# Attention with beacon keys and a maxout FFN: batch 0 cut at 512 queries, zeros between the first scores, a written order for batches 0 and 1

## The chip, the cores and the metric

The kernel runs on one core of a Trainium2 chip. Its engines are TensorE (PE, with its weight loads shown apart as PEld), VectorE (DVE), ScalarE (ACT), GpSimd (POOL) and SyncE (SP); each works through its own queue in order, and semaphores tie them together. The metric is the device time in microseconds of one execution. Beside it stands the span of one profiled execution, from its first to its last instruction.

## The reference

Two stages follow one another. Attention has 8 batches of 8 heads, 576 queries of 64 numbers, and 16 beacon keys and values that every query may see ahead of 576 causal ones:

```
k_all = np.concatenate([beacon_k, k], axis=2)
v_all = np.concatenate([beacon_v, v], axis=2)
scores = scale * np.matmul(q, k_all.transpose(0, 1, 3, 2))
scores = np.where(causal, -1000000000.0, scores)
a = softmax(scores)
attn_out = np.matmul(a, v_all)
```

The heads are then laid side by side, so that each of 4608 tokens has 512 numbers, and go through an FFN with three input matrices of 512 x 768 and one output matrix of 768 x 512:

```
h = np.maximum(np.maximum(x @ w1, x @ w2), x @ w3)
out = h @ w_out
```

Inputs and output are float32.

## The kernel before, in words

**Layout.** Matmuls are in bf16. Four heads make a quad (`HG = 4`), so there are two quads a batch and 16 in all, numbered Q. Queries and keys of a quad are loaded with a head on every 32 partitions, cast to bf16 (`cast_qk`) and transposed by DVE (`turn`, L197) into `qT` and `kT`, of which there are three each. The beacon keys of batch 0 come separately: POOL clears `first32` (L139), ACT's queue issues four small loads into it (L158), and DVE casts, transposes and copies them into `kT` (`turn_first_beacon_k`, L160). Those of batch 1 are loaded by SP after the values of batch 0 and turned by `turn_beacon_k` and `put_beacon_k`.

**Scores.** The 592 keys of a head are five tiles of 128, and a query needs only the tiles up to its own place. For each tile the columns are therefore the queries from a first one on, 1664 columns a quad. They are cut into bursts, or steps, that fill a PSUM bank of 512 columns for each of four heads. `emit_scores` multiplies a step's scores (L273; 32 rows of the array for each head, four heads at a time). ACT takes the exponential of two heads at once out of PSUM (L288, two instructions a step, which free the two `sc` tiles for the next step), and POOL zeroes what lies past the diagonal (`emit_masks`, L304). In batches 0 and 1 (`N_APART`) a quad has four steps of its own, of 496, 464, 336 and 368 columns, and in batch 0 the heads are multiplied in pairs. From batch 2 on the steps run on across quads, 3.25 a quad.

**Sums.** What this document calls the sums are the products of the exponentials with the values and, for the denominator, with a matrix of ones. In batches 0 and 1 `pv_pass` (L316) does one such product for half of the queries (288), into one of two PSUM banks; ACT turns a denominator into its reciprocal by a logarithm and an exponential (L344, L346), and DVE multiplies (scales) the two parts of the sums with it into `xT` (L350). From batch 2 on `pv_segment` does a third or two thirds of the queries at once (L387, L396 to L403).

**FFN.** A block is 512 tokens, so that block 0 consists of the first 512 of batch 0's 576 tokens. It has 18 input units of four matmuls (`mm1_unit`, L438; DVE takes the maximum over the three matrices in `hT`, L451) and then four output units of six matmuls (`mm2_unit`, L458). There are 198 units. `emit_ffn` emits the next one when the sums of its batch are done (`ready`) and the pace allows it: two a step during batch 1, 3.4 a step later.

**What sets the order.** The engines' queues hold the order in which the program emits, and this is written out: `begin` for the loads and batch 0's first quad, a table of steps (`at_step`) for loads, casts and transposes, and the loop in `emit_all` that puts scores, sums and units in turn. Before the first scores PE multiplies 17 times a matrix of zeros (`spare`, L545). In the loop, all of batch 0's sums are done at step 8 before the first FFN unit, and what is left of batch 1's before step 16 (`late`), the first of batch 2. The last output unit of all (`last_unit`) is done in two halves, whose copies and stores go over ACT and DVE with SP.

## Time and profile before

| | us |
|---|---|
| median of 3 runs | 287.48 |
| lowest, highest | 287.34, 288.59 |
| profiled execution, its own time | 286.83 |
| its span | 284.9 |
| busy: PE, DVE, ACT, POOL | 273.2, 171.4, 157.2, 88.4 |

In rows of the trace, the first two numbers are start and duration in us, counted from the first instruction. `out<-in` names what an instruction writes and reads, `x16` says that 16 of them were merged into one row, and brackets tell how long the engine had been idle before and for whom it waited. A merged row reaches from its first start to its last end, so other rows of the same engine can begin a little before it ends. In groups of instructions the columns are count, busy time in us, mean in ns, and idle time of the engine just before them with what ended it. `SPq`, `ACTq` and the like are an engine's own queue, where loads are issued. "Clock" is the share of TensorE's full clock that was granted.

### The profile page before, as it was taken

The numbers are of one execution on the slowest core, as the hardware profiler recorded it, in microseconds if no ns is written. First come the engines' busy times: TensorE is split into PE (matmuls) and PEld (weight loads), VectorE is DVE, ScalarE is ACT, GpSimd is POOL, SyncE is SP. The second block draws the span as 40 slices with busy tenths as digits, with TensorE's granted clock in tenths as the row PEclk, the third lists the DMA queues.
The fourth block names the chain that finished last, engine by engine and source line by source line (L and its number), as shares of the span: only waits on it lengthen the run. The fifth ranks groups of instructions, "written<-read, shape, count | busy, mean of one in ns | idle before, by whom it ended". The sixth has DMA issues, their size and how long they took to land.

```text
span 284.9 us, 7997 instructions
## 1 busy us (share of the span) xinstructions
PE 273.2 (96%) x3393; PEld 134.5 (47%) x3431; DVE 171.4 (60%) x298; ACT 157.2 (55%) x246; POOL 88.4 (31%) x165
## 2 busy tenths in 40 slices
PE   7699999999999999999999999999999999999995
PEld 3246444534545454445454545445454644444442
DVE  4727769856675766656656575666544465554553
ACT  5796576457784766556673686376647630210210
POOL 0483862235553523153415340442134100000000
PEclk9856999999999999999999999999999999999999
DMA  7999999689944954159056913380031003003004
GB/s 247 234 187 203 138 181 206 98 156 251 222 74 122 221 105 84 41 171 197 2 85 196 208 14 73 148 174 3 0 113 39 2 2 134 13 2 147 1 0 147
DMA packets 51923, 33.06 MB, mean 116 GB/s; under 512 B 41264, under 2 KB 42288, under 8 KB 51888
## 3 DMA queue, kind: packets, MB, share of 16 engines
q1 hardware_dynamic: 41152, 20.40, 27.6%
q0 software_dynamic: 10464, 12.01, 26.3%
q8 instruction: 26, 0.43, 0.6%
q10 hardware_dynamic: 272, 0.15, 0.2%
q14 instruction: 9, 0.07, 0.1%
HBM read 35.13 MB, written 9.44 MB: 156 GB/s over the span
## 4 chain that ended last, share of the span: by engine, by line
PE 91%; ACT 3%; issue 1%; DMA 1%; DVE 1%; ACTq 0%; DVEq 0%
PE fps L438 36%; PE sc L273 12%; PE fps L458 11%; PE pv L387 10%; PE pv L438 7%; PE sc L438 6%; PE pv L334 4%; ACT at_sb L288 3%; PE pv L458 2%; PE sc L458 2%; DMA first<-in_beacon_k_dram 1%; PE sc L387 1%; DVE xT L350 0%; ACTq L158 0%; DVE hT L451 0%
## 5 line engine op out<-in xcount | busy, mean ns | idle before, releaser
L288 ACT ACTIVATE at_sb<-sc 128x1024 bf16<-128x1024 f32 (+7 forms) x128 | 103.7, 861 | 31.8 <-PE sc L273 31.6
L438 PE MATMUL fps<-xT,w_sb 128*128 128x512 bf16 x447 | 113.3, 380 | 2.5 <-issue 1.6
L438 PEld LDWEIGHTS <-w_sb 128*128 128x128 bf16 x648 | 59.8, 98 | 74.5 <-issue 6.9
L304 POOL TENSOR_SCALAR_AFFINE_SELECT at_sb<-at_sb 128x512 bf16<-128x512 bf16 (+6 forms) x89 | 47.5, 551 | 127.4 <-ACT at_sb L288 119.0
L451 DVE TENSOR_TENSOR hT<-hT,fps 128x512 bf16<-128x512 bf16 x79 | 54.0, 685 | 33.9 <-PE fps L438 28.1
L273 PE MATMUL sc<-qT,kT 32*128 32x288 bf16 (+15 forms) x960 | 39.7, 266 | 2.9 <-ACT at_sb L288 2.5
L446 ACT CAST hT<-fps 128x512 bf16<-128x512 f32 x34 | 19.9, 586 | 29.9 <-PE fps L438 22.7
L458 PE MATMUL fps<-w_out_sb,hT 128*128 128x512 bf16 x144 | 34.7, 380 | 0.4 <-issue 0.3
L403 DVE TENSOR_TENSOR xT<-pv,recip 128x240 bf16<-128x240 f32 (+1 forms) x46 | 18.8, 450 | 25.5 <-ACT recip L398 24.9
L458 PEld LDWEIGHTS <-hT 128*128 128x128 bf16 x210 | 19.8, 98 | 25.6 <-DVE hT L451 1.7
L273 PEld LDWEIGHTS <-kT 32*128 32x128 bf16 x960 | 19.4, 94 | 22.3 <-issue 16.4
L396 ACT ACTIVATE lnd<-pv 128x240 f32<-128x240 f32 (+1 forms) x23 | 9.4, 408 | 29.8 <-PE pv L387 29.8
L466 DVE COPY y<-fps 128x512 f32<-128x512 f32 x25 | 17.3, 691 | 12.6 <-PE fps L458 12.2
L200 DVE STREAM_TRANSPOSE kT<-c 128x256 uint32<-128x256 uint32 (+1 forms) x32 | 22.0, 707 | 3.2 <-ACT c L193 3.1
L438 PE MATMUL pv<-xT,w_sb 128*128 128x512 bf16 x87 | 22.5, 379 | 0.2
L438 PE MATMUL sc<-xT,w_sb 128*128 128x512 bf16 x83 | 21.5, 380 | 0.1
L200 DVE STREAM_TRANSPOSE qT<-c 128x256 uint32<-128x256 uint32 (+1 forms) x32 | 21.5, 701 | 0.0
L387 PE MATMUL pv<-at_sb,v_sb 128*32 128x160 bf16 (+7 forms) x808 | 20.2, 243 | 0.0
L387 PEld LDWEIGHTS <-v_sb 128*32 128x32 bf16 (+1 forms) x864 | 16.3, 97 | 1.3
L226 POOL CAST v_sb<-vst 128x1024 bf16<-128x1024 f32 (+1 forms) x18 | 15.7, 894 | 0.5 <-issue 0.5
L451 DVE TENSOR_TENSOR hT<-hT,pv 128x512 bf16<-128x512 bf16 x15 | 10.3, 688 | 7.5 <-PE pv L438 4.1
L451 DVE TENSOR_TENSOR hT<-hT,sc 128x512 bf16<-128x512 bf16 x14 | 9.6, 687 | 7.6 <-PE sc L438 6.9
(54 smaller groups left out, 152.9 us busy)
## 6 DMA issues: line engine op xcount, KB each, us to landing
out_dram<-y SPq DMA_DIRECT2D x35, 256.0 KB, 2.0
vst<-in_v_dram SPq DMA_DIRECT2D x21, 256.0 KB, 4.8
c<-in_k_dram POOLq DMA_DIRECT2D x14, 288.0 KB, 4.9
c<-in_q_dram POOLq DMA_DIRECT2D x14, 288.0 KB, 6.0
w_sb<-in_moe_w_dram POOLq DMA_DIRECT2D x3, 768.0 KB, 8.6
vst<-in_v_dram SPq DMA_DIRECT2D x7, 224.0 KB, 3.5
vst<-in_v_dram SPq DMA_DIRECT2D x7, 160.0 KB, 6.9
w_out_sb<-in_moe_w_out_dram POOLq DMA_DIRECT2D x1, 768.0 KB, 10.1
```

What stands on the lines that cost most here:

```text
L200: nc.vector.transpose(dst.rearrange("p (t s) -> p s t", s=RUN)[:, s0:s1], src.rearrange("p (s d) -> p s d", d=DP),)
L226: cast(v_tiles[b][0:n, t0:t1].rearrange("p t h d -> p (t h d)"), stage["v", b][0:n, t0:t1].rearrange("p t h d -> p (t h d)"),)
L273: nc.tensor.matmul(sc[h // 2][:, h % 2, off : off + w], kT[hs, 128 * t : 128 * (t + 1), j], qT[hs, q0:q1, j], start=(j == 0), stop=(j == 1 ...
L288: nc.scalar.activation(out=at[Q][:, 2 * i : 2 * i + 2, a0 : a0 + w], in_=sc[i][:, :, off : off + w], func=AF.Exp, scale=scale,)
L304: nc.gpsimd.affine_select(out=view, in_=view, compare_op=ALU.is_ge, fill=0.0, base=q0 - (128 * t - Nb), pattern=[[0, HG], [1, edge - q0]], ...
L387: nc.tensor.matmul(pv_banks[32 * j : 32 * j + 32, c : c + w], lhsT, at_sb[0:r, j, a : a + w], start=(t == 0), stop=all(x[1] // BANK != c / ...
L403: nc.vector.tensor_mul(xT[:, 2 * g + part - 1, c0 : c0 + n], pv_banks[:, offs[part] : offs[part] + n], recip,)
L438: nc.tensor.matmul(ps[:, o0 : o0 + n], w_in[i][:, ct, 128 * ft : 128 * (ft + 1)], xT[:, ct, x0 : x0 + n], start=(ct == 0), stop=(ct == n_c ...
L446: nc.scalar.copy(hT[:, ft, :], ps)
L451: nc.vector.tensor_max(hT[:, ft, :], hT[:, ft, :], ps)
L458: nc.tensor.matmul(ps, hT[:, ft, 128 * tt : 128 * (tt + 1)], w_out_sb[:, ft, :], start=(ft == 0), stop=(ft == n_ft - 1),)
L466: nc.vector.tensor_copy(y, ps)
```

## The change

Batch 0's queries are cut at 512 (`TOKB`). Each of its two quads has three steps (`main`, 464, 496 and 384 columns) for the first 512 queries, which are all that FFN block 0 needs. The last 64 queries of both quads (`rest`, 320 columns a quad) are put into the steps behind them, which now run on without a gap through batch 1; batch 2 begins a new step. Its first step is number 14 (`N_FIRST`) instead of 16. Batch 1 uses whole quads and `pv_segment`, as the later batches do. The halves of `pv_pass` in batch 0 are 288 and 224 queries wide.

The sums of the last 64 queries of both quads are done together by a new function, `pv_rest`, in three passes (ones, then the two parts of the values) of 40 matmuls that are 64 columns wide.

All of the emission up to batch 2 is one written list. A letter stands for an action: S and E are a step's scores with its first exponential, and its second exponential with the masks; s and p a denominator and a sum of `pv_pass` (quad, half, part); r a pass of `pv_rest`; g and h a segment and its scaling; C a cast (quad, which, piece, and by ACT 0, DVE 1 or POOL 2); B and b beacon keys; t a transpose; k, v, w and n loads; c a cast of values; f the next FFN unit (with 1: its copy by DVE; with 2: in a third PSUM bank); x a number of multiplications with zeros, now 256 columns wide.

Smaller edits: `first32` is cleared by DVE; one staging buffer for values instead of two; reciprocals have a pool of four; the pace from batch 2 on starts at 22 units and is 3.2 a step instead of 3.4 once the second batch is through; the second half of the last output unit is copied half by ACT and half by DVE.

```diff
-    by_burst = [
-        [[(0, 0, HALF), (3, q_min[3], S)], [(1, q_min[1], S)], [(2, q_min[2], S)]]
-        + [[(0, HALF, S), (4, q_min[4], S)]],
-        [[(t, q_min[t], S) for t in range(n_kt)]],
-    ]
+    main = [[(0, 0, HALF), (1, q_min[1], HALF)]]
+    main.append([(2, q_min[2], HALF), (0, HALF, TOKB), (1, HALF, TOKB)])
+    main.append([(2, HALF, TOKB), (3, q_min[3], TOKB), (4, q_min[4], TOKB)])
+    rest = [[(t, TOKB, S) for t in range(n_kt)]]
+    whole = [[(t, q_min[t], S) for t in range(n_kt)]]
...
+    order = [(Q, main) for Q in range(n_quad)] + [(Q, rest) for Q in range(n_quad)]
+    order += [(Q, whole) for Q in range(n_quad, NQ)]
...
-    vst_pool = ctx.enter_context(tc.tile_pool(name="vst", bufs=2))
+    vst_pool = ctx.enter_context(tc.tile_pool(name="vst", bufs=1))
...
+    recip_pool = ctx.enter_context(tc.tile_pool(name="recip", bufs=4))
...
     for x in first32:
-        nc.gpsimd.memset(x, 0.0)
+        nc.vector.memset(x, 0.0)
...
+    def pv_rest(part):
+
+        n_r = S - TOKB
+        if part == 0:
+            bank = pv_pool[0].tile([128, 512], FP32, name="pv")[:, 0 : 3 * n_quad * n_r]
+            rest_tiles.append(bank.rearrange("p (g c n) -> p g c n", g=n_quad, c=3))
+        ps = rest_tiles[0]
+        for Q in range(n_quad):
+            for t in range(n_kt):
+                a = next(a + TOKB - q0 for q0, q1, a in at_piece[Q, t] if q0 <= TOKB < q1)
+                n = k_rows[t]
+                for j in range(HG):
...
+                    nc.tensor.matmul(
+                        ps[32 * j : 32 * j + 32, Q, part],
+                        lhsT,
+                        at[Q][0:n, j, a : a + n_r],
...
-        if i == 0 and tb > 0:
+        if i == 0 and (tb, ft) in by_vector:
+            nc.vector.tensor_copy(hT[:, ft, :], ps)
+        elif i == 0:
             nc.scalar.copy(hT[:, ft, :], ps)
-        elif i == 0:
-
-            nc.vector.tensor_copy(hT[:, ft, :], ps)
...
-            (nc.scalar.copy, nc.vector.tensor_copy)[half](y[:, cols], ps[:, 0:MH])
-            (nc.scalar, nc.sync)[half].dma_start(out[c0 : c0 + 128, cols], y[:, cols])
+            pieces = ((0, MH // 2), (MH // 2, MH)) if half else ((0, 0), (0, MH))
+            for (a, b), copy, queue in zip(
+                pieces, (nc.scalar.copy, nc.vector.tensor_copy), (nc.scalar, nc.sync)
+            ):
+                if a < b:
+                    copy(y[:, m0 + a : m0 + b], ps[:, a:b])
+                    queue.dma_start(out[c0 : c0 + 128, m0 + a : m0 + b], y[:, m0 + a : m0 + b])
...
     def spare(n):
-
         ps = ffn_psum.tile([128, TOKB], FP32, name="fps")
         for _ in range(n):
-            nc.tensor.matmul(ps, zeros[:, 0:128], zeros, start=True, stop=True)
+            nc.tensor.matmul(ps[:, 0:256], zeros[:, 0:128], zeros[:, 0:256], start=True, stop=True)
...
-        spare(17)
...
+        orders = (
+            "C 0 1 0 0; x 29; C 0 0 1 0; x 2; C 0 1 1 1; B 0; t 0 1 1; t 0 1 0; C 0 0 0 2; t 0 0 "
+            "1; t 0 0 0; C 1 1 2 0; C 1 0 2 1; x 3; S 0; E 0; t 1 0 1; t 1 1 0; k 2 0; x 7; B 1; "
+            "S 1; t 1 1 1; t 1 0 0; x 5; c 0 2; c 2 4; k 2 1; E 1; k 3 1; c 4 5; S 2; E 2; x 3; w "
+            "0; t 2 0 1; s 0 0; S 3; v 1 0 1; x 1; E 3; s 0 1; x 3; b 2; x 1; S 4; E 4; p 0 1 1; "
+            "x 1; t 2 1 0; p 0 1 2; S 5; p 0 0 2; w 1; E 5; v 1 1 2; k 3 0; s 1 0; p 0 0 1; s 1 "
+            "1; p 1 1 1; w 2; w 3; p 1 0 2; S 6; E 6; k 4 0; p 1 0 1; p 1 1 2; t 2 1 1; f; t 2 0 "
+            "0; f 1 2; v 1 2 3; f; S 7; t 3 1 1; f; E 7; f 1 2; f 1; r 0; v 1 3 4; S 8; E 8; n; "
+            "f; t 3 0 1; v 1 4 5; f; r 1; t 3 0 0; b 3; S 9; f; t 3 1 0; r 2; f 1 2; k 4 1; k 5 "
+            "1; E 9; f 1; f 1; g 2 0; S 10; h 2 0; f; f; E 10; f 2; S 11; t 4 0 0; f 1; f 2; f; k "
+            "5 0; E 11; t 4 0 1; S 12; t 4 1 1; E 12; g 2 1; h 2 1; S 13; b 4; f; E 13; g 3 0; t "
+            "4 1 0; h 3 0; f; f 1; g 3 1; h 3 1 "
+        )
...
-        ready = -1
-        allowed = 0.0
...
-        first_rate, rate = 2.6, 3.4
+        emit_first()
+        ready = 1
+        allowed = 22.0
+
+        first_rate, rate = 2.6, 3.2
```

More of the change, by code (lines that the diff above doesn't have):

```diff
@@ L580 @@
[L580 to L603 removed]
+    exps = {}
@@ L605 @@
+    for Q in range(N_APART, NQ):
+        b, g = divmod(Q, n_quad)
+        if g == 0:
             at_step(first_step[Q] + 1, L(load_v, b))
```

272 lines of the change are left out of this document (147 added, 125 removed).

## The prediction

> **What bounds the kernel now.** I read the page's busy shares first, then a table of stages, then the chain that ended last, and only then single instructions of the opening.
>
> ```profile
> PE 273.2 (96%) x3393; PEld 134.5 (47%) x3431; DVE 171.4 (60%) x298; ACT 157.2 (55%) x246; POOL 88.4 (31%) x165
> ```
>
> TensorE (PE) is busy for 96% of the span: work taken from other engines pays only where PE waits for them. Where that is, the stages show (columns: stretch, its length, busy time and instructions of PE, PEld, DVE, ACT, POOL; granted clock; DMA share; GB/s).
>
> ```profile
> 5.98:9.39 3.41, 2.19 (x23) 1.02 (x22) 2.45 (x8) 1.68 (x3) 0.00 (x0) 1.00 0.96 328
> 9.39:12.80 3.41, 2.25 (x19) 0.56 (x21) 2.23 (x6) 3.41 (x6) 2.04 (x3) 1.00 1.07 180
> 16.22:19.63 3.41, 3.29 (x42) 1.24 (x41) 0.64 (x2) 3.22 (x6) 2.64 (x5) 0.50 1.10 196
> 23.04:26.46 3.42, 3.28 (x72) 2.11 (x64) 2.83 (x6) 1.48 (x3) 1.43 (x3) 0.50 1.07 200
> 29.49:54.34 24.85, 24.64 (x340) 11.69 (x344) 20.04 (x37) 14.14 (x22) 14.16 (x25) 1.00 1.20 165
> 54.34:281.40 227.06, 223.96 (x2741) 110.42 (x2766) 135.52 (x224) 121.29 (x193) 61.77 (x115) 1.00 0.42 97
> ```
>
> From 29.49 us, the first FFN unit, PE has no time to give: 24.64 of 24.85 us, then 223.96 of 227.06. Everything rearranged lies before 54.34, where batch 2's scores begin. Between 12.80 and 26.46 the clock was halved, and yet ACT was busy 3.22 of 3.41 us in the middle of it: the exponentials were nearly the bound there, so a full clock would not have halved that stretch. The chain gives the opening's joints.
>
> ```profile
> 2.36 3.90 DMA first<-in_beacon_k_dram
> 6.40 0.20 DVE first L161
> 7.78 0.63 PE sc L273 x15
> 29.49 1.68 PE fps L438 x7
> ```
>
> The first beacon keys land at 2.36 + 3.90 = 6.26, VectorE (DVE) casts them at 6.40, scores start at 7.78, and the FFN 21.7 us later.
>
> **The change, part by part.** The order of the work is rewritten up to batch 2, so I place its milestones one by one and compare at one common point: batch 2's first scores. At that point the old kernel (54.34) has done 18 FFN units. The new order has done the same scores and sums of batches 0 and 1, and 21 units (its string holds 21 f), three of them 4-per-block output units. What is left afterwards is then alike, so the new kernel breaks even if it gets there three output units later.
>
> ```profile
> 46.52 0.99 PEld L334 LDWEIGHTS <-v_sb 128*32 128x32 bf16 x40 [0.42 <-issue]
> 38.06 0.62 PE L273 MATMUL sc<-qT,kT 32*128 32x288 bf16 x16
> 38.61 1.69 PE L438 MATMUL fps<-xT,w_sb 128*128 128x512 bf16 x7
> 48.07 1.90 PE L438 MATMUL fps<-xT,w_sb 128*128 128x512 bf16 x7
> 49.90 0.90 PE L334 MATMUL pv<-at_sb,ones 128*32 128x288 bf16 x32
> 70.95 0.34 PE L387 MATMUL pv<-at_sb,ones 128*32 128x240 bf16 x8
> 71.54 0.65 PE L273 MATMUL sc<-qT,kT 32*128 32x144 bf16 x24
> 73.95 0.74 PE L387 MATMUL pv<-at_sb,ones 128*32 128x336 bf16 x20
> 75.75 0.65 PE L273 MATMUL sc<-qT,kT 32*128 32x176 bf16 x24
> 276.42 1.29 PE fps L458 x6
> ```
>
> An output unit is 1.29 us (last row), so break-even is 54.34 + 3 x 1.29 = 58.2.
>
> *Start of the scores.* The beacon's cast, transpose and copy move ahead of all four transposes of quad 0 in DVE's queue, and the memset that the beacon's load waits for moves from POOL behind four small memsets of DVE (I allow up to 0.3 us).
>
> ```profile
> 5.21 0.78 DVE L200 STREAM_TRANSPOSE kT<-c 128x320 uint32<-128x320 uint32 x1 [0.34 <-ACT c L193]
> 5.91 0.66 DVE L200 STREAM_TRANSPOSE qT<-c 128x256 uint32<-128x256 uint32 x1
> 6.40 0.19 DVE L161 CAST first<-first 128x64 bf16<-128x64 f32 x1
> 6.96 0.77 DVE L200 STREAM_TRANSPOSE qT<-c 128x320 uint32<-128x320 uint32 x1
> 8.58 0.76 DVE L193 CAST c<-st 128x1152 bf16<-128x1152 f32 x1 [0.86 <-DMA st<-in_k_dram]
> L193 ACT CAST c<-st 128x640 bf16<-128x640 f32 x2 | 1.4, 725 | 0.5 <-DMA st<-in_k_dram 0.3 <-DMA st<-in_q_dram 0.2
> ```
>
> Today three transposes run while the beacon is on its way and one follows, to 7.73. In the new order DVE stands at the beacon until 6.40, with the four transposes queued behind it, whose inputs are cast by then. Beacon 6.40 to 6.96; then starts 0.70 apart after a 320-wide (5.91 - 5.21) and some 0.57 after a 256-wide one (0.66 less the same overlap of 0.08): 6.96 + 0.70 + 0.57 + 0.70 + 0.65 = 9.58, scores at 9.63. That is **1.85 us later**. Could the beacon land early? Nothing in the change issues it sooner, so no gain; if those 0.3 us carry through, 2.15. I take 1.85. The cast of quad 1's keys goes to ACT ahead of its first exponential; its data land just before 8.58, and at ACT's 0.725 for 640 columns it takes at most 1.3 us for 1152, so ACT is free at 9.9, before the first scores are done (9.63 + 0.65 = 10.28). It costs nothing, but it also means that an early beacon would win back only 0.4.
>
> *The exponentials of batch 0.* Two quads of 928, 992 and 768 columns, twice each, instead of 992, 928, 672 and 736.
>
> ```profile
> 8.43 6.51 ACT L288 ACTIVATE at_sb<-sc 128x992 bf16<-128x992 f32 x8 [1.58 <-PE sc L273]
> L288 ACT ACTIVATE at_sb<-sc 128x768 bf16<-128x768 f32 x12 | 9.7, 809 | 0.0
> L288 ACT ACTIVATE at_sb<-sc 128x992 bf16<-128x992 f32 x8 | 7.5, 992 | 2.9 <-PE sc L273 2.9
> L288 ACT ACTIVATE at_sb<-sc 128x928 bf16<-128x928 f32 x8 | 7.2, 943 | 2.6 <-PE sc L273 2.6
> L346 ACT ACTIVATE recip<-lnd 128x288 f32<-128x288 f32 x8 | 3.5, 444 | 0.3
> ```
>
> Eight in a row took 6.51, about 0.05 each less than their means add up to. Two quads: 4 x (0.89 + 0.945 + 0.76) = 10.4; the two reciprocals of quad 0 lie among them, 0.8 and 0.7. Sum 11.9: from 10.28 to 22.2. PE's scores and zeros fit under it at full clock: a 256-wide zero is half of a 512-wide matmul (1.29 / 6 / 2 = 0.11), seven of them 0.75, and with a score step under 0.8 PE has 1.6 us of work in ACT's 1.8. The causal masks on POOL run beside it.
>
> *From there to the first FFN unit.* The sums of quad 0 cannot be scaled by DVE before the beacon keys of batch 1 are turned, which stands ahead of them in DVE's queue.
>
> ```profile
> bk<-in_beacon_k_dram SPq DMA_DIRECT2D x1, 4.0 KB, 4.7
> 21.78 0.18 DVE L149 CAST bk<-bk 128x64 bf16<-128x64 f32 x1
> 11.90 1.76 POOL L304 TENSOR_SCALAR_AFFINE_SELECT at_sb<-at_sb 128x448 bf16<-128x448 bf16 x3
> L350 DVE TENSOR_TENSOR xT<-pv,recip 128x288 bf16<-128x288 f32 x16 | 6.7, 451 | 6.4 <-PE pv L334 6.4
> ```
>
> The eighth of these loads is issued at 16.6 and lands 4.7 us later, 21.3; I take 21.0, as POOL's first weight load is issued behind it instead of ahead. Cast, transpose and copy take 0.8. Behind them wait the multiplies of quad 0, 0.4 to 0.45 each, with a transpose between, and behind these PE's sums, which alternate over two PSUM banks: quad 1's first denominator at 23.1, when the second multiply has freed its bank; the second at 23.95, after the first one's logarithm; its reciprocal by 25.2; then the last four multiplies one after another, 27.05. First FFN unit at **27.1**. Without the beacon's wait the last masks bound it (three took 1.76, these are narrower: some 1.4 after 22.2), and with the same steps behind them it is 26.5; with no wait for banks either, 25.5. I take 27.1, since the load has its row.
>
> *From the first FFN unit to batch 2.* Eighteen units of 0.86 and three of 1.29, 19.4, in nine groups that each cost 0.11 more (a pair takes 49.90 - 48.07 = 1.83): 20.4. Seven score steps at 0.55 (38.61 - 38.06): 3.85. Batch 1's sums in segments, 2 x (0.59 + 1.80): 4.8. The last 64 queries: three passes of 40 matmuls 64 wide. No row shows these. From below they cost their columns, ten sets of four at 27 ns, 0.27, with a change of shape 0.45; from above 40 weight loads at the pace of 46.52, 0.99. I take 0.75, nearer the loads: 2.25 (1.35 to 3.0). Sum 31.3. So batch 2 starts at 27.1 + 31.3 = 58.4, **0.2 later** than break-even. In other words: from the scores to the FFN it is 17.5 us instead of 21.7, of which the late start takes back 1.85 and the deferred queries 2.25.
>
> *The zeros and the clock.* The first 34 zeros have as many columns as the old 17 and start after two more memsets of DVE: from about 1.6 to 7.6. Then PE is empty until 9.63. What does the clock react to? The last two of these rows are of the scores alone (PE, PEld, clock).
>
> ```profile
> 1.47 6.05 PE L545 MATMUL fps<-xT 128*128 128x512 bf16 x17 [1.47 <-DVE xT L539]
> ...
> 5.98:9.39 3.41, 0.65 (x16) 0.53 (x17) 1.00 0.96 328
> 9.39:12.80 3.41, 2.25 (x19) 0.56 (x21) 1.00 1.07 180
> ```
>
> PE was as busy in the stretch after which the clock fell (2.25) as in the one after which it held (2.19); the former held only scores on 32 rows, the latter 1.5 us of zeros on the whole array. And 3.28 us of sums (23.04) raised it, 3.29 us of scores and sums (16.22) did not. So array work counts, not busy time. New work in such stretches: 1.5 us of zeros in 5.98 to 9.39, less than before; scores with zeros to 19.6; and, while the sums wait for the beacon of batch 1, about 0.5 us in 19.6 to 23.0, less than in the stretch that lost the clock. A fall there makes the sums before the first FFN unit twice as long and costs about 0.7; a rise one stretch later ends it. Bounds: nothing (it holds) to 5 (below). I take 0.3 to 0.4, between the two that I hold likely.
>
> [...]
>
> *Other edits.* The last output unit's final copy, which ends the chain, is split over two engines.
>
> ```profile
> 281.65 0.42 DVE y L486
> ```
>
> Half of it, less a fixed part: -0.1. One staging buffer for values instead of two is hidden, since batches are 6.5 steps apart and casts follow their loads by three. The pacing of 3.2 instead of 3.4 units a step only shifts units between a loop and a tail that are both full of PE work (223.96 of 227.06): 0, from -1 to +1.
>
> Sum: 0.2 + 0.35 - 0.1 = +0.5. The profiled execution took 286.83 (span 284.9), 0.65 under the median of 287.48; the difference carried to the median gives **288.0**.
>
> **The rivals.** *Faster.* The sums are not held by beacon and banks: first FFN unit at 25.5 (-1.6), the narrow passes at their lower bound (-0.9): 0.2 - 1.6 - 0.9 - 0.1 = -2.4, 285.1. For it: the beacon's load could land earlier, with a weight load less ahead of it. Against: DVE's strict order.
>
> *Slower: the zeros do not hold the clock.* It falls at 9.4 after 2.2 us of empty PE. Then seven zeros take 1.5 us and a score step 1.5, against 1.8 of exponentials: PE becomes the bound and the zeros lengthen it. By the same steps batch 0's exponentials end 1.9 later, the sums add 1.6, and one stretch of FFN at half speed 1.7: up to +5.2, 293; with two of the three some 290.5. It decides if the fall comes before 12.8 and lasts two stretches. Against: zeros fill the array, so they should raise the clock again.
>
> *The clock never falls.* The zeros and the sums are enough everywhere, PE's longest gap being the 2 us before the scores: +0.1, 287.6. For it: 1.5 us of zeros held the clock once (5.98). Against: the thin stretch before the FFN. [...]
>
> **How the numbers follow.** A measurement of this kernel can tell about 0.5%, 1.4 us, from no change. Forecast, one short fall at some phase of the clock's stretches: 0.34, 286.6 to 288.9. No fall: 0.11. Faster rival: 0.28. Slower rival: 0.27. The range takes in both ends until 2 in 10 are out: 284.8 to 291. A little of the forecast's own spread lies beyond the 1.4 us, so faster 0.29, same 0.43, slower 0.28.
>
> **What would show it.** Right: first scores near 9.6, DVE idle before the beacon's cast; ACT unbroken to 22; first FFN unit near 27; batch 2's first scores at 58 to 59; a narrow pass near 0.75. Wrong: scores at 7.8, a first FFN unit before 26 or after 29, a clock of 0.5 from 9.4, or a different length from batch 2 to the end.

## The result and the profile after

The changed kernel takes **291.88 us** (median of 6 runs, 291.61 to 292.40), against 287.28 for the kernel before in the runs beside it: a ratio of **1.0162, 95% interval 1.0135 to 1.0189**. It is slower by 4.6 us, where 288.0 was forecast and 291.0 was the end of the range. Its profiled execution took 291.63, with a span of 289.9, 5.0 more than the span before.

The page's busy times, and the table of stages (columns as before: stretch, length, PE, PEld, DVE, ACT, POOL, clock, DMA share, GB/s):

```profile
PE 277.6 (96%) x3741; PEld 140.9 (49%) x3741; DVE 169.5 (58%) x301; ACT 159.1 (55%) x252; POOL 89.5 (31%) x168
```

```profile
7.70:11.12 3.42, 1.71 (x31) 1.40 (x34) 2.18 (x4) 2.37 (x3) 0.00 (x0) 1.00 1.20 232
11.12:14.53 3.41, 3.41 (x42) 1.94 (x38) 3.31 (x9) 2.53 (x3) 2.78 (x5) 0.50 0.97 207
14.53:17.94 3.41, 3.41 (x62) 1.97 (x56) 1.56 (x3) 3.02 (x5) 2.56 (x6) 0.50 1.06 160
17.94:21.36 3.42, 3.42 (x97) 2.54 (x90) 0.78 (x1) 3.39 (x6) 3.09 (x5) 1.00 1.04 171
21.36:24.77 3.41, 1.08 (x32) 0.89 (x32) 1.94 (x7) 1.57 (x3) 2.78 (x6) 1.00 1.05 182
24.77:28.18 3.41, 3.36 (x120) 2.93 (x116) 1.38 (x4) 1.60 (x4) 2.47 (x4) 0.50 1.43 186
29.14:61.09 31.95, 30.91 (x564) 15.49 (x557) 21.79 (x40) 19.07 (x33) 11.63 (x22) 1.00 0.88 143
61.09:286.40 225.31, 224.01 (x2756) 109.00 (x2748) 133.54 (x223) 122.06 (x194) 63.40 (x118) 1.00 0.44 97
```

TensorE is as busy as before by its share, so the loss is again to be found in single places. The clock is halved behind two thin stretches (1.71 and 1.08 us of work): from 11.12 to 17.94, and from 24.77 to 28.18, where PE is busy for 3.36 of 3.41 us. In both thin stretches PE waits, and the first three of these rows say for what:

```profile
9.28 0.62 PE L281 MATMUL sc<-qT,kT 32*128 32x288 bf16 x16 [2.48 <-DVE qT L210]
22.76 0.20 DVE L161 CAST bk<-bk 128x64 bf16<-128x64 f32 x1 [2.46 <-DMA bk<-in_beacon_k_dram]
23.85 0.41 PE L342 MATMUL pv<-at_sb,v_sb 128*32 128x288 bf16 x12 [1.76 <-DVE xT L358]
29.14 1.04 PE L469 MATMUL fps<-xT,w_sb 128*128 128x512 bf16 x4
40.06 0.22 PE L281 MATMUL sc<-qT,kT 32*128 32x32 bf16 x8 [0.81 <-issue]
```

The first scores come at 9.28 and the first FFN unit at 29.14, 0.35 earlier than before. Batch 2's first scores come at 61.09, where 58.2 was break-even: 2.9 us lost. From there on I compare the start of every score step in both kernels, less the FFN units by which they differ, at 0.86 and 1.29 us each. This **debt** is 2.9 for five steps, 3.9 at the seventh, 4.2 at the tenth, 5.2 at the eleventh, and then stays between 4.8 and 5.2 to the end. So 2.9 us are lost in the opening, some 1.1 where batch 2's sums begin, 1.0 at the tenth step, and nothing in the 180 us behind.

```profile
77.15 1.04 POOL L234 CAST v_sb<-vst 128x1024 bf16<-128x1024 f32 x1 [2.98 <-DMA vst<-in_v_dram]
78.24 0.50 PE L433 MATMUL pv<-at_sb,v_sb 128*32 128x240 bf16 x16 [0.63 <-POOL v_sb L234]
97.28 3.52 PE L469 MATMUL fps<-xT,w_sb 128*128 128x512 bf16 x14 [0.50 <-DVE xT L449]
```

The same two places in the kernel before, where the cast of the values had ended 1.2 us ahead of their use, and output units stood in the step with the gap:

```profile
68.85 1.04 POOL L226 CAST v_sb<-vst 128x1024 bf16<-128x1024 f32 x1 [0.50 <-issue]
71.12 0.49 PE L387 MATMUL pv<-at_sb,v_sb 128*32 128x240 bf16 x16
88.37 2.54 PE L458 MATMUL fps<-w_out_sb,hT 128*128 128x512 bf16 x11 [0.16 <-issue]
```

### The profile page after: what moved, and what is told of

The parts are those of the page before. It is cut to its first block, busy times and chain, and to the rows that moved or that the text cites. A ratio compares the mean times of both kernels' runs of the same rounds, so it can differ in the third digit from the quotient of the medians.

```text
span 289.9 us, 8670 instructions
## 1 busy us (share of the span) xinstructions
PE 277.6 (96%) x3741; PEld 140.9 (49%) x3741; DVE 169.5 (58%) x301; ACT 159.1 (55%) x252; POOL 89.5 (31%) x168
## 3 DMA queue, kind: packets, MB, share of 16 engines
q1 hardware_dynamic: 41296, 20.47, 27.1%
q0 software_dynamic: 10464, 12.01, 26.5%
## 4 chain that ended last, share of the span: by engine, by line
PE 80%; DMA 8%; SPq 5%; DVE 2%; ACT 2%; issue 1%; POOL 0%; DVEq 0%; POOLq 0%
PE fps L469 31%; PE fps L488 12%; PE pv L433 10%; PE sc L281 8%; PE pv L469 7%; PE sc L469 7%; SPq L226 3%; DMA vst<-in_v_dram 3%; PE sc L488 2%; DMA st<-in_q_dram 2%; DMA bk<-in_beacon_k_dram 2%; SPq L158 2%; PE pv L488 1%; PE pv L342 1%; DMA st<-in_k_dram 1%
## 5 line engine op out<-in xcount | busy, mean ns | idle before, releaser
L469 PE MATMUL fps<-xT,w_sb 128*128 128x512 bf16 x444 | 110.3, 380 | 0.5 <-DVE xT L449 0.5
L312 POOL TENSOR_SCALAR_AFFINE_SELECT at_sb<-at_sb 128x512 bf16<-128x512 bf16 (+8 forms) x94 | 49.1, 541 | 129.2 <-ACT at_sb L296 126.3
L449 DVE TENSOR_TENSOR xT<-pv,recip 128x240 bf16<-128x240 f32 (+1 forms) x54 | 22.1, 451 | 33.5 <-ACT recip L444 33.4
L281 PE MATMUL sc<-qT,kT 32*128 32x80 bf16 (+21 forms) x1104 | 37.8, 252 | 3.7 <-DVE qT L210 2.5
L488 PE MATMUL fps<-w_out_sb,hT 128*128 128x512 bf16 x162 | 38.3, 380 | 0.0
L469 PE MATMUL pv<-xT,w_sb 128*128 128x512 bf16 x116 | 29.8, 379 | 0.1
L433 PE MATMUL pv<-at_sb,v_sb 128*32 128x160 bf16 (+7 forms) x952 | 24.0, 243 | 0.7 <-POOL v_sb L234 0.6
L210 DVE STREAM_TRANSPOSE qT<-c 128x320 uint32<-128x320 uint32 (+1 forms) x32 | 21.5, 702 | 2.6 <-DMA c<-in_q_dram 2.5
L210 DVE STREAM_TRANSPOSE kT<-c 128x320 uint32<-128x320 uint32 (+1 forms) x32 | 22.1, 706 | 1.3 <-DMA c<-in_k_dram 1.3
L433 PE MATMUL pv<-at_sb,ones 128*32 128x336 bf16 (+4 forms) x372 | 14.4, 268 | 0.0
## 6 DMA issues: line engine op xcount, KB each, us to landing
c<-in_q_dram POOLq DMA_DIRECT2D x14, 288.0 KB, 5.9
c<-in_k_dram POOLq DMA_DIRECT2D x14, 288.0 KB, 4.7
```

Of the source, the lines that this page charges most:

```text
L210: nc.vector.transpose(dst.rearrange("p (t s) -> p s t", s=RUN)[:, s0:s1], src.rearrange("p (s d) -> p s d", d=DP),)
L281: nc.tensor.matmul(sc[h // 2][:, h % 2, off : off + w], kT[hs, 128 * t : 128 * (t + 1), j], qT[hs, q0:q1, j], start=(j == 0), stop=(j == 1 ...
L312: nc.gpsimd.affine_select(out=view, in_=view, compare_op=ALU.is_ge, fill=0.0, base=q0 - (128 * t - Nb), pattern=[[0, HG], [1, edge - q0]], ...
L433: nc.tensor.matmul(pv_banks[32 * j : 32 * j + 32, c : c + w], lhsT, at_sb[0:r, j, a : a + w], start=(t == 0), stop=all(x[1] // BANK != c / ...
L449: nc.vector.tensor_mul(xT[:, 2 * g + part - 1, c0 : c0 + n], pv_banks[:, offs[part] : offs[part] + n], recip,)
L469: nc.tensor.matmul(ps[:, o0 : o0 + n], w_in[i][:, ct, 128 * ft : 128 * (ft + 1)], xT[:, ct, x0 : x0 + n], start=(ct == 0), stop=(ct == n_c ...
```

## The experiments

All ratios are against the kernel before on the same chip, with 95% intervals. All kernels compute the whole reference. Diffs of the written list show only the words around an edit. The expectations speak of twenty zeros between the scores; there are 21.

### What holds the first FFN unit: batch 1's beacon keys

`e1_b2_late` turns the beacon keys of batch 1 behind batch 0's last multiply instead of ahead of its first.

```diff
-s 0 1; x 3; b 2; x 1; S 4; ... p 1 0 1; p 1 1 2; t 2 1 1;
+s 0 1; x 3; x 1; S 4; ... p 1 0 1; p 1 1 2; b 2; t 2 1 1;
```

> The beacon keys of batch 1 are cast and turned behind batch 0's last multiply instead of ahead of its first, so DVE no longer stands at their load (which lands at 22.49) with four multiplies queued behind it. My theory: this wait is what delays the first FFN unit. The masks on POOL end with batch 0's exponentials near 23; the multiplies and the two banks then set the pace, and the first FFN unit comes at 27.5 instead of 29.14, batch 2's first scores 1.5 earlier (59.6), the whole 1.5 under the changed kernel's 291.9: 290.4. Rival 1 (the wait only covers others: last masks, logarithms, the two banks, a halved clock): less than 0.5, 291.4 to 291.9. Rival 2 (the keys are then late for quad 2's scores at step 7, which need them): no gain at the FFN but a new wait at step 7, 291.9 or more.

Measured: 289.66, ratio 1.0078 (1.0041 to 1.0114), clear of the changed kernel's 1.0162: 2.4 us gained, more than the 1.5 expected. The first unit comes at 28.45 and batch 2 at 59.55. `e18_again` is the changed kernel unchanged.

> The changed kernel once more, beside the others on the same chip, with a profile of its own: how far the places of its losses vary from execution to execution. Its wait at batch 1's beacon keys should be there again (1.8 before, 4.2 in e3_no_zeros), as should the late values of batch 2 (0.8 to 1.3) and the 1.0 at the tenth step; a stall at a code block's end only where TensorE gets through one in less than about 6 us. The time 1.014 to 1.018 of the kernel before.

Measured: 293.01, ratio 1.0179 (1.0129 to 1.0230). Its waits between 8 and 62 us (who waited for whom: total, times, longest):

```profile
DVE bk L161 <- DMA bk<-in_beacon_k_dram: 4.8, 1, 4.8
PE pv L342 <- DVE xT L358: 4.8, 2, 4.7
```

The keys land at 24.6 here instead of 22.5, TensorE waits 4.7 us instead of 1.8, and the first unit comes at 31.12. The wait is shown as a cause, and its size varies from one execution to the next: the two figures, with 4.2 in `e3_no_zeros`, lie on both sides of the 2.4 that the runs lose to it. In the changed kernel's own chain (start, us, what) one of the eight issues of these keys holds SP's queue for 1.68 us, where most take 0.42, and the last load is on its way for 4.79; in `e18_again`, issued at the same time (17.72), it takes 6.9.

```profile
15.50 1.68 SPq L158
17.69 4.79 DMA bk<-in_beacon_k_dram
```

Behind the wait the clock was halved as well, from 24.77 to 28.18 in the changed kernel and from about 22.3 to 29.2 in `e18_again`. The last 184 matmuls ahead of the first unit, without their waits, took 4.05 to 4.2 us at full clock (e8, e10, e11 and e12, all below), and 4.9 in these two, where the clock was halved for 3.4 us of them. In `e18_again` the 1.0 at the tenth step and the late values (1.1) were there again.

### A wait that no name is given for: blocks of code

In `e1_b2_late` TensorE got to step 6 three microseconds earlier (24.32 for 27.63), and then stood still in it for 1.78 us, for nothing that the profile names. `e2_gap_zeros` and `e8_b2_zeros` both put twenty zeros more (forty instructions, with their weight loads) ahead of the first scores, in the changed kernel and in e1.

```diff
-x 29; C 0 0 1 0; x 2;
+x 29; C 0 0 1 0; x 22;
```

> Twenty more multiplications with zeros (about 2.2 us at full clock) go into the stretch from 6.8 to 9.0 in which TensorE is empty before the first scores. Theory of the prediction (array work in a stretch of 3.41 us decides the next one's clock): the stretch from 7.70 to 11.12 is then filled, the clock stays at 1.00 from 11.12 to 14.53, batch 0's exponentials end 0.5 to 1.0 earlier, the whole 291.0 to 291.5. Rival (the fall at 11.12 has another cause, or ACT is the bound there at either clock): clock 0.50 from 11.12 as before, or the same time within 0.3: 291.6 to 292.2. Against both: if the zeros run past the arrival of quad 0's queries, the first scores start later by as much.

> Batch 1's beacon keys turned late, as in e1_b2_late, and twenty more zeros ahead of the first scores, as in e2_gap_zeros. In e1 TensorE stands still for 1.78 us at 26.34, behind eight matmuls of step 6, for nothing that the profile names. That is its 706th recorded instruction; the changed kernel's unexplained 0.81 at 40.06 is its 1218th, exactly 512 later, and one packet of 16 KB of instructions, 256 of them, went over the DMA engines 2.3 us before in each. Theory (TensorE waits for its code, which is fetched in blocks of 256 instructions over the loaded DMA engines): forty more instructions ahead move the block's end forty instructions earlier in the program; the stall comes again at the 706th, now in the middle of the last sums of batch 0, at about 26, and the first FFN unit stays at 28.3 to 28.9. Rival (step 6 waits for something of its own, keys or a score tile): the stall stays behind the eighth matmul of step 6, the 746th. The whole: about as e1 or 0.3 less, 289.3 to 289.7.

Measured: e2 292.09, ratio 1.0155 (1.0090 to 1.0219), so nothing gained: the sums still wait 1.8 us behind the keys. The clock did not fall at 11 in its profile, but it did not in that of `e18_again` either, without the zeros. e8 292.52, ratio 1.0134 (1.0080 to 1.0188), slower than e1 by its median (the intervals overlap). In its profile batch 2 starts as early as e1's (59.32 and 59.55); its debt grows behind that, by 3.4 where the values come late, and the clock is halved once there (78.74 to 82.15). How many matmuls (first count) and weight loads (second) had been done when PE stopped is seen in a table of stages that ends there; behind it stands the first row after the stop. In e1:

```profile
0.00:26.34 26.34, 18.82 (x351) 13.51 (x352) 14.21 (x34) 16.82 (x24) 14.65 (x28) 0.99 1.01 213
```

```profile
26.34 0.37 PE L281 MATMUL sc<-qT,kT 32*128 32x64 bf16 x13 [1.78 <-issue]
```

In e8:

```profile
0.00:31.41 31.41, 25.83 (x479) 18.24 (x480) 17.41 (x43) 19.95 (x30) 16.15 (x31) 1.00 1.00 207
```

```profile
31.42 0.41 PE L281 MATMUL sc<-qT,kT 32*128 32x64 bf16 x12 [0.99 <-issue]
```

In `e10_pace24` (below), two of its stops:

```profile
0.00:27.31 27.31, 20.67 (x351) 14.36 (x352) 13.15 (x34) 16.82 (x24) 13.39 (x28) 0.88 0.95 206
0.00:39.15 39.15, 31.89 (x607) 19.98 (x608) 20.17 (x49) 24.91 (x39) 18.89 (x36) 0.91 1.03 205
```

```profile
27.32 0.37 PE L281 MATMUL sc<-qT,kT 32*128 32x64 bf16 x25 [0.87 <-issue]
39.16 0.22 PE L281 MATMUL sc<-qT,kT 32*128 32x32 bf16 x8 [0.26 <-issue]
```

And in the changed kernel, whose row at 40.06 with 0.81 was shown above:

```profile
0.00:40.06 40.06, 32.49 (x607) 20.90 (x608) 20.83 (x50) 25.21 (x39) 19.75 (x38) 0.87 1.08 208
```

351, 479 and 607 matmuls, always 128 apart, with a weight load each: 703, 959 and 1215 instructions, steps of 256, whatever work stands there. The expectation for e8 missed in one point: its stop did not come at 351 again, but at 479, in the scores of step 7, while the rival's place, behind the eighth matmul of step 6, was passed without one. The transfers of e1 between 23.9 and 24.2 name what comes (queue: packets, MB, share of the engines), and the page of e1 how much of it there is in all:

```profile
q0 software_dynamic: 27, 0.06, 98.0%
q8 instruction: 1, 0.02, 20.0%
```

```profile
q8 instruction: 29, 0.48, 0.7%
```

0.48 MB for TensorE's 2 x 3741 instructions are 64 bytes each, and 256 of those are the 0.02 MB of one packet. The page's 29 packets are also as many as the block ends that PE passes in 3741 matmuls, and at each stop shown here one had started 2.2 to 2.5 us before PE went on. So I take it that PE waits for its own code, which comes in blocks over DMA engines that the loads already fill (98.0% in the view of e1 above). e10's two stops are two blocks and 11.84 us apart, 5.9 a block; over all runs it was, in the opening, 4.9 (`e20_all_again`) to 6.9 us (`e9_b2_loads`) from one block end to the end of a stop at the next. An estimate from these: 128 matmuls that take less than some 39 to 54 ns each are through before the next block is there. The longest stop in the opening was 1.91 us (`e9_b2_loads`); from 61 us on, the list of TensorE's waits in the changed kernel has none for `issue`. The 0.81 at 40.06 in the changed kernel is of this kind.

### The late values, and the step without a ready unit

`e5_loads` issues quad 6's queries and keys behind step 12 and no longer at step 14, together with quad 7's and ahead of the values. `e9_b2_loads` joins this with e1.

```diff
-S 12; t 4 1 1; E 12; g 2 1;
+S 12; t 4 1 1; E 12; k 6 1; k 6 0; g 2 1;
...
-        if Q > N_APART + 1:
+        if Q > N_APART + 2:
```

> Quad 6's queries and keys are loaded behind step 12 of the written list instead of at step 14, where today quad 6's, quad 7's and the values of batch 2 are issued together and the values, issued last, land at 75.9 to 81.2. Theory: the values of batch 2 land some 4 us earlier, POOL casts them before TensorE needs them (it waits 0.63 for the cast at 78.24, and its weight loads wait 0.85 and 0.22), the debt stays at 2.9 instead of rising to 4.2 by step 8, and the whole takes 290.8. Rival 1: the waits are gone, but the next ones (the FFN's ready units, which run out two steps later) take their place: 291.6 to 292.0. Rival 2: quad 6's early loads delay a load or a cast of batch 1 in turn, and batch 2 starts later.

> The edits of e1_b2_late and e5_loads together. If the wait for the beacon keys and the late values are two causes that add up, 289.66 - 1.1 = 288.5, and no wait for the cast of batch 2's values. If the code's block bounds the opening instead of the beacon keys (the rival to the first of the two), its gain is the loads' alone over the changed kernel with an undisturbed clock: 289 to 290. If the loads, now earlier, delay something of batch 1: 289.7 or more.

Measured: e5 289.99, ratio 1.0114 (1.0031 to 1.0196); e9 289.92, ratio 1.0074 (1.0049 to 1.0099). The rows of e5 that answer to 77.15 and 78.24 above:

```profile
74.93 1.04 POOL L234 CAST v_sb<-vst 128x1024 bf16<-128x1024 f32 x1 [0.81 <-DMA vst<-in_v_dram]
77.39 0.49 PE L433 MATMUL pv<-at_sb,v_sb 128*32 128x240 bf16 x16
```

The cast is two microseconds earlier and TensorE does not wait. In every profile with this edit and the pace of 2.6 the debt stays flat up to the eighth step; in every one without the edit it rises by 1.1 to 3.4 before the seventh. This loss is shown in the trace. The times say less: alone the edit gained 1.4 us with a wide interval, on top of e1 nothing that can be told (1.0074 against 1.0078; 288.5 us was expected), and e9's profile shows a longer stop for code, 1.91, and later first scores, 9.82.

The third loss is the tenth step: all 44 ready units are done, and the next need xT. `e4_pace` allows 2.2 units a step instead of 2.6 in the changed kernel, `e10_pace24` 2.4 in e9. `e19_hold` keeps the pace and holds back one unit in `e14_all`, below.

```diff
-        first_rate, rate = 2.6, 3.2
+        first_rate, rate = 2.2, 3.2
```

```diff
             allowed += rate if ready > 1 else first_rate
+            if k < N_FIRST + 9:
+                allowed = min(allowed, 43.9)
```

> The pace of the FFN in the steps before batch 1's sums are all in goes from 2.6 to 2.2 units a step, so fewer units have been used up when the ready ones run out at the tenth step of the late stage (TensorE's wait of 0.50 at 97.28, with 36 input and 8 output units done). Theory: the 0.9 us lost between steps 8 and 10 (debt 4.23 to 5.15) goes, and the whole takes 290.9 to 291.1. Rival 1: with less FFN work between them the scores wait for the exponentials instead, which costs as much at steps 1 to 8: 291.6 to 292.2. Rival 2: the 0.9 is a matter of what unit stands where, and the units left over lengthen the tail by nothing: 291.9.

> As e9_b2_loads, and the pace is 2.4 units a step instead of 2.6 until batch 1's sums are in: by the eighth step 22 + 9 x 2.4 = 43.6 units are allowed, so that one of the 44 ready ones is left for the step in which TensorE waits 0.50 for xT and loses 1.0 in all. With 2.2 (e4_pace) that loss was gone, but a unit waited 1.2 for VectorE's maximum behind two transposes. Theory: the loss at the tenth step goes and the new wait does not come: 0.7 to 1.0 under e9_b2_loads, 287.5 to 288. Rival: any thinner pace brings the wait for the maximum back: the same as e9 or up to 1.2 more.

> e14_all, but up to the ninth step of the late stage at most 43 of the 44 ready FFN units are started, so that one output unit is left for the tenth step, whose sums make the next ones ready; the pace stays as it is everywhere else. Theory (the 1.0 lost at the tenth step is the wait for xT with no unit to fill it): the debt does not rise there, the whole is 0.7 to 1.0 under e14's, 0.9995 to 1.002. Rival (as with the thinner pace of e10_pace24, the place of the gap only moves, here to the ninth step, which has a unit less): the same as e14, 1.003 to 1.005.

Measured: e4 293.03, ratio 1.0234 (1.0158 to 1.0310); e10 292.03, ratio 1.0150 (1.0112 to 1.0189), 2.1 over e9; e19 288.43, ratio 1.0024 (1.0003 to 1.0046), the same as its base. In all three the debt does not rise at the tenth step (5.7 to 5.7, 3.2 to 3.2, 1.6 to 1.7), so the cause is right. But it comes back elsewhere: in e4 as this wait at the fourth step, since fewer units leave a bank waiting for VectorE's maximum behind two transposes,

```profile
PE pv L469 <- DVE hT L481: 1.2, 1, 1.2
```

in e10 as 1.3 up to the ninth step and 0.8 far behind, in e19 as 0.55 between the steps 17 and 28. So the rivals were right that the loss only moves; e10 lost more than the 1.2 that its rival allowed.

### The start of the scores, and loads out of the way

On top of e9, `e11_b0_last` turns batch 0's beacon keys behind three of the four transposes, and `e12_v_late` issues batch 1's first values behind the weights.

```diff
-C 0 1 1 1; B 0; t 0 1 1; t 0 1 0; C 0 0 0 2; t 0 0 1; t 0 0 0;
+C 0 1 1 1; t 0 1 1; t 0 1 0; C 0 0 0 2; t 0 0 0; B 0; t 0 0 1;
```

```diff
-S 3; v 1 0 1; ... E 5; v 1 1 2; ... S 6; E 6; k 4 0;
+S 3; ... E 5; ... S 6; E 6; v 1 0 1; v 1 1 2; k 4 0;
```

> As e9_b2_loads, and the first beacon keys are cast, turned and copied behind three of quad 0's four transposes instead of ahead of all of them. The prediction charged their place with 1.85 us of later scores. Theory of the prediction: the first scores come at 8.2 to 8.6 instead of 9.8, ACT's first exponential at 9.2 instead of 10.4 (its cast of quad 1's keys ends there), and if the exponentials carry it on, the whole is 0.7 to 1.2 under e9's. Rival (the stretch behind is bound by what the DMA engines bring: beacon keys, code and the first weights, which land at 27.5): the first FFN unit stays at 28.3 to 29, the whole is that of e9 within 0.5.

> As e9_b2_loads, and the first two loads of batch 1's values (16 beacon rows, 112 and 128 key rows), today issued at 18.3 and 23.6 between the weights' loads, come behind the last of the weights. Nobody needs them before 44. Theory (the DMA engines are full from 6 us on, so code blocks, beacon keys and weights wait in line): the second weights land 1 to 2 us earlier than 34.0, the code block behind the 705th instruction comes up to 0.5 earlier, the whole is 0.3 to 0.8 under e9's. Rival (code and weights wait on something other than the line): no difference, within 0.3 of e9. If batch 1's values are then late for its first sums at 44: 0.5 or more over e9.

Measured: e11 289.29, ratio 1.0080 (1.0051 to 1.0109); e12 289.68, ratio 1.0095 (1.0067 to 1.0123): both as e9. In e11 the scores start 1.44 earlier than in e9, but ACT's first exponential only 0.2:

```profile
8.38 0.62 PE L281 MATMUL sc<-qT,kT 32*128 32x288 bf16 x16 [0.92 <-DVE qT L210]
9.18 1.15 ACT L205 CAST c<-st 128x1152 bf16<-128x1152 f32 x1 [1.84 <-DMA st<-in_k_dram]
10.24 0.94 ACT L296 ACTIVATE at_sb<-sc 128x928 bf16<-128x928 f32 x1
```

It waits behind the cast of quad 1's keys, which land late in this execution. Where the same edit stands in `e14_all` and `e20_all_again`, the first exponential comes at 9.35 and 9.50, against 9.90 in the changed kernel; e11's time shows nothing of it. In e12 the weights come faster, as the median time to landing of its three weight loads shows, and below it that of e9:

```profile
w_sb<-in_moe_w_dram POOLq DMA_DIRECT2D x3, 768.0 KB, 9.9
```

```profile
w_sb<-in_moe_w_dram POOLq DMA_DIRECT2D x3, 768.0 KB, 12.7
```

The stop for code shrinks from 1.91 to 0.25 and the first unit comes at 26.15, the earliest but one of all. The gain is lost again before batch 2 (59.42): more stops of 0.26 and 0.65, and 1.40 at 59.27, again for nothing named. By their weight loads (some matmul records are missing there) all three stand at block ends.

### The zeros between the scores

`e3_no_zeros` takes them out of the changed kernel, `e13_few` out of e9; `e15_narrow` puts them back into e13 with 16 columns instead of 256; `e16_wide_first` makes the 34 zeros ahead of e13's scores 18, most of them 512 wide.

```diff
-x 7; B 1; ... x 5; c 0 2; ... E 2; x 3; w 0; ... x 1; E 3; ... x 3; b 2; x 1; S 4; ... x 1; t 2 1 0;
+B 1; ... c 0 2; ... E 2; w 0; ... E 3; ... b 2; S 4; ... t 2 1 0;
```

```diff
-x 29; C 0 0 1 0; x 2; ... x 3; S 0;
+x 14 512; x 1; C 0 0 1 0; x 1 512; ... x 1 512; x 1; S 0;
```

> The changed kernel without the twenty zeros between batch 0's scores and first sums; the 34 ahead of them stay. Theory of the prediction (array work in a stretch holds the clock): without them the clock falls in the first stretch behind the first scores and stays down for two or three, to the first sums; batch 0's exponentials end up to 1.9 later, the whole 292.5 to 295. Rival 1 (ACT and the beacon's load set the pace there at either clock; in the changed kernel's runs a clock of 0.982 and one of 0.994 took the same 289.9 to 290.4): no difference, 291.5 to 292.4. Rival 2 (the zeros themselves are in the way of the scores): faster, 290.5 to 291.3.

> As e9_b2_loads without the twenty zeros between batch 0's scores and sums (e3_no_zeros was 0.5% faster than the changed kernel with a clock halved for six stretches instead of three). Theory (the zeros buy clock in a stretch that ACT and the DMA engines bound anyway, and cost TensorE's time and forty instructions of code): 0.5 to 1.5 under e9's, clock 0.97, the code's stall gone or moved forty instructions on. Rival (with the beacon wait gone, TensorE is near the bound before the first unit, so the halved clock now costs): 0.5 to 2 over e9's.

> As e13_few, with the 21 zeros between the scores back in their places, but 16 columns wide instead of 256: the instructions of e9_b2_loads without their time on TensorE. Without any of them the kernel was 0.9 to 1.5 us faster than with them (1.0042 against 1.0074 of the kernel before). Theory A (TensorE goes through its code no faster than a block of 256 instructions in 5.9 to 6.9 us while the DMA engines are full, so 42 instructions cost about 1 us): as slow as e9, 1.007. Theory B (it is their time: they stand ahead of scores and sums that exponentials wait for): as fast as e13, 1.004. Theory C (the clock): it falls as in e13, 0.97 to 0.98, so a time like e9's could not be the clock's.

> As e13_few, and the 34 zeros ahead of the first scores become 18, 16 of them 512 columns wide, as in the kernel before: the same columns in 32 instructions less. Theory A (a count of instructions that have to be fetched by the first unit): 0.4 to 0.7 under e13, 1.002. Rival (the first blocks lie ready before the kernel starts, and the place of a block's end only moves): within 0.3 of e13, 1.0035 to 1.005.

Measured: e3 290.46, ratio 1.0106 (1.0071 to 1.0142); e13 288.46, 1.0042 (1.0021 to 1.0062); e15 289.92, 1.0097 (1.0063 to 1.0130); e16 290.38, 1.0097 (1.0061 to 1.0134). Without the zeros both kernels are faster by their medians, by 1.6 and 0.9 us (the ends of the intervals overlap), although the clock is lower (e13's runs list 0.970 to 0.982, e9's 0.986 to 1.000). With the zeros' instructions but next to none of their time (seven took 0.33 us in e15, and 0.94 at 256 columns in e11), e15 is slow again, at the same low clock; its interval just misses e13's (1.0063 and 1.0062), and the two ran on different chips. So TensorE's time is hardly what the zeros cost, and their instructions are likely. A mere count it is not either: e16 has 32 fewer than e13 and is slower, with stops of 1.21 and 0.84 at block ends, as e15 has of 0.42 and 0.92. That the place of the block ends decides fits all four, but it is not shown: in e13's own profiled execution TensorE waited 5.6 us for batch 0's last values, as in no other, so its stops could not be compared.

This does not make the clock worthless. In one and the same kernel a lower mean clock goes with a longer time: in some 90 executions of the kernel before, beside these experiments, the median was 286.9 us at 0.979 to 0.985, 287.7 at 0.973 to 0.979 and 288.4 below that, 0.7 to 0.8 for every stretch more at half clock (3.41 x 0.5 / 286 is 0.006). Which of the two brings on the other these lists do not tell; but the 184 matmuls ahead of the first unit, which took 4.05 to 4.2 us at full clock, took 5.9 in e4 and e5 and 6.3 in e15, nearly all of it at half clock.

### All edits together

`e14_all` joins e11, e12 and e13, `e20_all_again` repeats it; `e17_best` has batch 1's first values between the input and the output weights, and the zeros of e16.

> All edits of e11_b0_last, e12_v_late and e13_few together: beacon keys of batch 0 behind three transposes, those of batch 1 behind batch 0's sums, quad 6's and the first values' loads moved, no zeros between the scores. If the three add up as their theories say, 1.5 to 3 under e9's 289.9, which is about the kernel before or just under it (ratio 0.995 to 1.002). If the DMA engines bound the stretch up to the first FFN unit whatever the order (rival), 1.004 to 1.008 as e9 and e1.

> e14_all once more, beside e19_hold on the same chip: its 1.0038 again (1.002 to 1.006) if the edits bring it, 1.007 or more if that was chance. Its profile shows whether stalls at the ends of code blocks are again absent, as their places in the program predict, or come where TensorE gets through a block in less than about 6 us.

> e14_all with batch 1's first values issued between the third input weights and the output weights instead of behind both (their late landing at 40 to 41 cost 0.6 there), and the zeros ahead of the scores in 18 instructions as in e16_wide_first. From e14's 1.0038: 0.3 to 0.6 for the values, 0 to 0.6 for the zeros: 1.000 to 1.003. What is left is the 1.0 at the tenth step of the late stage, where no unit is ready. If e14's sum of small gains was luck of the beacon keys' and the code's landing: 1.004 or more.

Measured: e14 288.13, ratio 1.0038 (1.0022 to 1.0054), between what was expected (up to 1.002) and its rival (1.004 or more); e20 287.93, 1.0024 (1.0006 to 1.0043); e17 289.23, 1.0075 (1.0044 to 1.0107), where 1.000 to 1.003 was expected. Three quarters or more of the loss is undone, and the sum holds in a second execution; no version beat the kernel before. In e20 the first unit comes at 26.56 and batch 2 at 58.28, break-even to 0.1 us; what is left is the 1.0 at the tenth step. e17 stops for 0.95 and 0.84 at other block ends, and is 0.4% slower than e14 by its median. Its clock is halved for five stretches in that profile, up to 30.35, so that the block ends are not shown to be the whole cause.

## Why the prediction was wrong

- **Start of the scores**, 9.63 with DVE at the beacon keys: measured 9.28, with that wait. Right as a time. As a cost, 1.85 was too much: with the beacon keys behind three transposes the first exponential came 0.4 to 0.55 earlier (9.50 and 9.35 in e20 and e14, for 9.90), near the 0.4 that the prediction itself allowed, and in e11 not at all.
- **Batch 0's exponentials** until 22.2: measured 22.93, with the clock halved for two stretches behind 11.12; 21.95 and 22.05 in e1 and e18 without that. Right.
- **From there to the first FFN unit**, the step that failed first. That the sums wait for batch 1's beacon keys was in the working, and e1 confirms it. The term that was too small is the landing of these keys: 21.0 was forecast, 22.49 and 24.6 measured, so the first unit came at 29.14 and 31.12 instead of 27.1. For 21.0 the last of the eight loads had to be issued near 16.3; it was issued at 17.69, since one issue before it held SP's queue for 1.68 us. Its 4.8 us from issue to landing were as forecast in this profile, and 6.9 in e18. That is 1.5 of the 2.0; the rest is no more than what the halved clock behind the wait took (4.9 us for the last 184 matmuls, for 4.05 to 4.2). And my floor without that wait, 26.5, did not hold in e1 (28.45), where the code's block took its place; in e20, which stops for 0.35 only, it did (26.56).
- **To batch 2** 31.3, measured 31.95. A narrow pass took 0.42, not 0.75, which saves 1.0; two stops for code (0.13 and 0.81) were not in the list of costs at all. The new kernel has 3741 matmuls instead of 3431 (so many weight loads; the old page's 3393 matmuls lack 38 records), most of the new ones narrow and in the opening, and I priced them by columns and weight loads alone.
- **After batch 2's start 0**, the other step that failed: 2.1. One staging buffer is indeed hidden, but the loads' order is not: quads 6 and 7 stand ahead of batch 2's values, and the cast came when TensorE already waited. And 18 against 21 units was booked at three output units' full 3.9 us, though units done early were missing at the tenth step: 1.0 of it was worth nothing.
- **The pacing of 3.2** at 0, from the eleventh step on: right.
- **The zeros and the clock**, +0.35 for one short fall: the clock was halved in three stretches, behind the two thin ones. The fall at 11.12 cost nothing that can be told, since the keys bound what follows, and e18 without it was no faster. The fall at 24.77 is the one that the prediction named, in the sums before the first FFN unit, and its price of about 0.7 holds (0.7 to 0.9 in those 184 matmuls). The whole time did not show it: runs of the changed kernel with a mean clock of 0.982 and of 0.994 took 291.6 and 292.1. The zeros cost 0.9 to 1.6 in all, by a way I had not seen. In the changed kernel the clock fell behind idle gaps of 2.48 and 1.76 us of TensorE. That array work decides it, and not busy time, was my inference from four stretches of the profile before, and the runs do not show it: without the zeros between the scores the clock was halved for six stretches in e3 and for five in e13, but for two in `e14_all` and three in `e20_all_again`.
- **The rivals.** The slower one came nearest in time, by the wrong cause. Its condition came true in part, a fall before 12.8 that lasts two stretches (11.12 to 17.94, though not from 9.4), but batch 0's exponentials ended 0.7 later than forecast and not 1.9, and no stretch of FFN ran at half clock. The faster one, without waits for keys and banks, asked for a first unit at 25.5; e20's opening, with its waits taken out by edits, comes to 26.56, and the rest of the loss keeps it from winning.

## What to carry to other kernels

With the DMA engines full, as in this opening (a share of 0.97 to 1.43 in the stretches from 7.70 to 28.18 us of the changed kernel), one small load took 4.8 us from issue to landing in one execution and 6.9 in the next, and an issue ahead of it 1.68 instead of 0.42. So forecast both the issue and the landing of such a load with a margin, and put whatever waits for it in an engine's strict order last, or ahead of nothing that is urgent. Instructions are loads too (29 packets and 0.48 MB in the changed kernel): here dense narrow matmuls outran their own code, as I read these stops, and stood still for up to 1.91 us, so count them in blocks where the profile shows a wait for "issue". And a head start in one stage is worth its full price only if the following stage has enough ready work to use it.

## What the runs showed of the hardware that I had not expected

With the DMA engines full (a share of 0.95 to 1.08 up to the stops shown), TensorE stood still at places whole steps of 256 of its instructions apart, for 0.13 to 1.91 us; from one block end to the end of a stop at the next it was 4.9 to 6.9 us in the opening (5.9 twice running in e10, 6.5 in the changed kernel from 33.59 to 40.06). A program got slower by 0.5% with 21 matmuls that cost next to no time of their own (e15 against e13, on two chips; seven of them took 0.33 us). In the same kernel, the beacon keys of batch 1 landed between 22.5 and 24.6 us from one execution to the next. The granted clock, down to half for up to six stretches of 3.41 us (e3), does not rank different kernels: e13 with 0.970 to 0.982 was faster than e9 with 0.986 to 1.000. Within one kernel it went with the time, 0.7 to 0.8 us a stretch in the kernel before, and the matmuls ahead of the first FFN unit took half as long again where all of them ran at half clock (e4, e5, e15).
